# Routing attention and a SoLU feed-forward on one core: the first pair of heads prepared by thirds of its tokens, in a new written order

## The chip, the cores and the metric

The kernel runs on one core of one Trainium2 chip. The metric is the device time of one execution in microseconds (us); less is better. A core has TensorE (PE in the profile, its weight loads PEld), VectorE (DVE), ScalarE (ACT), GpSimd (POOL) and SyncE (SP), which here only issues DMAs. Each engine works through its own instructions in the order in which they were written and waits for the others by semaphores.

## The reference

q, k and v have 4 batches, 8 heads, 768 tokens and 64 numbers a head. Each query and each key is given the nearest of 16 centroids of its head; a query attends only to keys with its own centroid. The result, 3072 rows of 512, goes through a feed-forward block.

```python
q_assign = argmax(einsum('bhsd,hcd->bhsc', q_n, c_n)); k_assign = ...   # normalised rows
mask = q_assign[..., :, None] == k_assign[..., None, :]
attn = softmax(where(mask, q @ k.T / 8, -1e9));  x = attn @ v           # per batch and head
h = x @ w_in;  solu = h * softmax(h)
out = (solu - mean) / sqrt(var + 1e-6) * g_ln @ w_out
```

## The kernel before

**Layout.** Heads go in pairs: 4 batches x 4 pairs. For a pair, `qk` holds for queries and for keys 64 rows of numbers and, beneath them, rows with the one-hot of the token's centroid, so that one product gives the score and, where the centroids agree, a large constant, which the exponential's bias takes off again. `scores` (L595, the matmul is L602) fills a PSUM bank `sps` of up to 512 columns, `expo` (L608) takes its exponential on ACT into `e`, `values` (L625) multiplies 128-column blocks of `e` by v with a column of ones, and `normalise` (L637, L650) divides on DVE into `x`. Rings of three score banks and nine `e` tiles tie the three engines together.

**A pair's preparation.** In batches 1 to 3 a pair is loaded in 128-byte runs and turned by DVE (L408). In batch 0 it is loaded with tokens on partitions, turned on PE (`turn_tokens`, L387) and copied out of PSUM (`keep_tokens`, L394; steps `tp` and `xa`). Then `cast` (L432 to L436, `ca`) writes bf16 rows into `qk`; `clusters` (L446, L451, `cl`) multiplies by the centroids; DVE turns the products (`turn_back`, L460, `tb`), takes the maximum (L473, `mx`), compares (L479, L485, `oh`), turns back (L492, L495, `ot`), and `place` (L507 to L515, `pl`) copies the one-hot rows into `qk`.

Pairs 1 to 3 of batch 0 ("apart") are loaded whole in 1536-byte runs, two neighbouring tokens lying side by side, so that after the turn one half of the partitions holds even tokens and the other odd tokens; their centroids `c_by_two` stand accordingly, and each head's one-hot takes 16 rows.

Pair 0 of batch 0 is the first work of all. It is taken by halves of its tokens (`halves_of`), each half of each head by a DMA of 96 KB in 256-byte runs, eight in all on the ACT and SP queues (L370). It uses the centroids `c_bd`, 32 one-hot rows copied twice, `blank` (L524) to clear one head's rows, and its scores are units of kind "C": 384 queries by 128 keys, 24 banks of 384 columns. All other units of batch 0 are of kind "A": 256 queries, banks of 512 columns.

The centroids are scaled on DVE (L843 to L856) after one `pow` on POOL, and turned on PE twice: step `cp` for `c_bd` (L876), and later `cq` for `c_by_two` (L869).

**Feed-forward.** For each of 24 tiles of 128 tokens: x is turned by DMA (`tx`, L680), four `h` steps (L711) multiply by w_in (loaded by `li`, cast by `wi`, L553), `hm` (L717, DVE maximum), `ex` (L723, ACT exponential), `u` (L730, DVE product), `tu` (L735, turned by DMA), `bn` and `ag` (L741, L745, DVE), `at` and `al` (L751 to L760, POOL), four `y` steps (L775) and `sc` (L790, L792). `ce` (L588) centres w_out once.

**What sets the order.** Every step is added to a list by `add` with an engine, a cost, a due time, and what it needs. The order of each engine is not found by those: the strings `ORDER` name, engine by engine, the kinds of steps in sequence (S scores, E exponentials, V values, N normalise, ld, lv, lo and li loads of q/k, v, w_out and w_in, fl a filler matmul with no use for its result, and so on), and `AWAY` says which steps run on another engine than their first. `run` issues the steps in that order. PE begins with `wm`, six fillers of 512 columns (L820).

Of the kernel before, what the change touches and what calls it, by code (L numbers as in the profile page):

```python
# [22 lines left out]
class Weave:  # L23
# [6 lines left out]
        ld4 lv si ld4 lv lg ld4 lv2 ld4 lo2 ld4 lo ld3 lo ld3 li4 tx ld3 lv3 tx ld4 tu ld9 lv ld tu  # L30
        tx ld3 tu ld3 ou ld2 ou ld tu ld12 tu ld4 lv ld2 ou tx ld3 tu ou ld2 tx lv ld tu ld4 tx ld
        tu ou2 ld lv ld4 tu ld4 tu ld ou ld7 pl ou ld lv2 ld3 tu lv tx ou tu lv pl ld4 ou2 tx lv tu
        tx ou tu pl2 tu2 tx tu tx ou2 tx ou tu tx2 ou tu2 ou2 tu2 ou6
    """
    ORDER["POOL"] = """
        po z ca2 pl2 cv z bl pl2 ca z ca pl2 ca z2 ca3 cv ca cv ca pl3 sg ca cv2 pl3 ca2 gs pl ca cv
        ca wi ca pl2 wi3 bl ca pl2 cv at cv pl ca pl al bl at cv ca pl ca pl cv ca3 al at ca al ca
        at ca pl2 bl cv pl2 ca4 at ca2 al ca pl2 bl pl2 cv2 ca3 al at pl2 bl pl2 ca pl al ca3 at cv
        at pl ca pl2 ca2 pl al cv2 bl cv2 pl2 ca pl al pl at al at pl2 ca3 at al bl cv pl2 bl cv2
        ca3 pl5 al cv3 at al ca2 cv ca cv ca2 at ca2 pl ca al pl2 at2 pl3 at ca cv al at2 al2 at2 al  # L40
        at al3 at al2 at2 al2
    """
    ORDER["PE"] = """
        wm tp2 cp tp cl tp fl5 cl fl4 S3 tp2 S2 tp S cq S tp S2 tp2 S2 V3 S cl S tp2 V3 S gt S tp S
        tp S2 cl S2 V2 S V S2 tp S2 tp S2 V2 S V S2 cl S2 V2 S V2 S3 V S2 V2 S2 V S cl S3 su S2 V3 S
        V S3 V3 S2 V S su S2 V S V3 S3 me S3 V4 S3 cl S3 V4 S2 h S h S2 h S h S2 V3 S2 V h S h V S V
        S h S V S V S h S2 V3 S2 V h S2 h V2 S y3 S2 h3 S3 y V3 h V S2 V2 S cl S3 h2 S2 V3 S y2 S V
        h2 S V y2 S h S V h S2 h S y3 S2 y V3 h S3 cl V2 S V S y S2 y2 S3 V3 S y S2 V3 S2 cl S V S2
        V2 S h S2 V2 S V S h S2 V2 cl V2 S3 y2 S V S2 V y S2 y V2 S3 h2 S V h S h S2 V h S V S V y2
        S h V y2 S2 V S h3 S cl V S2 V2 S h V cl S3 h2 V y V S3 y2 V S h V3 S y S h S2 h2 S3 V2 y h  # L50
        S V S2 y V3 y S3 h3 y S3 V3 S h S V S V cl S V S h S cl V2 S3 y V2 S y S2 y V2 S3 h y V S3 V
        h V2 S3 cl S2 V2 S y3 S2 y S V3 S V S y S2 V S V3 S2 y2 S3 y V2 S2 h V2 S3 h3 S V S2 V y S V
        h2 V2 S y S2 y V y S h2 S3 cl h V S2 V3 S h V2 S3 h2 S y S2 V h S2 V y2 V4 S3 y h S2 h V h V
        S V S y2 S3 V3 h2 S2 h2 S2 y2 S V S h2 S V3 S2 h S h S2 V S y V2 S V y2 S2 h2 S2 h2 V2 S2 V2
        y S2 h V2 h V S2 h S V h S3 V2 h y S V y3 V h3 S2 y3 S2 y h2 V2 h y h y3 h V h V y4 h ptx h
        y4 h2 y3 h2 y ptu2 y6 ptu y ptu y5
    """
    ORDER["DVE"] = """
        cn cb xa ca tb mx oh ot pl2 tb mx oh ot xa3 bl cf cv xa zo xa2 tb ca mx oh gk N ot tb pl mx
        xa2 oh xa cv N ot tb pl N xt mx xt N oh ot tb pl2 ca N pl xt mx N sk oh N ot xt ce3 N tb ce5  # L60
        N hm mx N u oh ot bn N bn ag hm xt2 u N bn2 hm ag sc xt u N bn tb hm mx bn oh ag u xt bn ot
        xt N cv hm bn ag sc xt tb mx N u xt oh ot sc N bn2 xt ag xt tb N hm mx tb N oh ot u xt mx N
        bn oh bn xt hm ot ag N cv u bn2 xt hm tb mx u N tb oh mx hm ot bn2 oh ag u N sc ag hm bn ot
        u bn N xt2 ag xt2 hm tb N bl mx tb bn2 oh u N xt ag xt sc hm ot tb mx oh N bn sc N u bn N ag
        xt ot bn ca N mx sc oh hm u bn ag N xt hm bn2 bl tb u ot ag N hm mx bn2 u bn N oh ot hm bl2
        u ag N cv hm sc bn u N hm ag bn N bn u bn2 hm ag2 N bn u bn2 N ag hm bn u N ag hm bn2 u bn2
        hm sc u N ag2 bn tx hm bn sc u bn ag hm bn tu ag u2 bn2 ag sc
    """
    ORDER["ACT"] = """
        wa xa2 ca2 xa ca2 E12 xa2 E6 xa E58 ex E12 ex E8 ex E8 ex E3 sc E5 ca E2 ex E25 ex E9 sc E6  # L70
        ex E5 sc E2 ex E9 ex E8 ex E9 sc E6 ex E18 ex E21 ex E5 sc E3 ex E9 ex E7 sc E2 ex E7 ex E8
        ex E7 ex E6 sc E ex E2 sc E3 ex E2 sc ex sc ex sc ex tu sc tu2 sc2 oz
# [3 lines left out]
        ca0.0.0.0.0 ca0.0.0.1.1 ca1.3.1.1 sc23.0 tu22.1 tu23.1 xa0.0.1.0 xa0.2.1.0 xa0.2.1.1  # L76
        xa0.3.0.0
    """.split(), "ACT"))
    AWAY.update(dict.fromkeys("""
        bl0.0.1 bl2.2 bl3.1 bl3.2 bl3.3 ca0.0.1.0.0 ca0.1.1.0 ca1.0.0.1 ca3.1.1.0 cv0.0.0 cv0.2.0  # L80
        cv1.2.0 cv2.0.0 cv3.3.0 pl0.0.0.1.1 pl0.1.0.0 pl0.2.1.1 pl0.3.0.0 pl0.3.0.1 pl0.3.1.0 sc0
        sc10 sc13 sc17 sc19 sc2 sc23.1 sc3 sc6 sc8 sc9 tu22.0 zo
    """.split(), "DVE"))
    AWAY.update(dict.fromkeys("""
        ca0.0.1.1.1 pl0.0.0.1.0 pl0.0.1.0.0 pl0.0.1.1.0 pl1.0.0.0 pl1.0.0.1 pl1.0.1.0 pl1.0.1.1
        pl1.1.0.0 pl1.1.0.1 pl1.1.1.0 pl1.1.1.1 pl1.2.0.0 pl1.2.0.1 pl1.2.1.0 pl1.2.1.1 pl1.3.0.0
        pl1.3.0.1 pl1.3.1.0 pl1.3.1.1 pl2.0.0.0 pl2.0.0.1 pl2.0.1.0 pl2.0.1.1 pl2.1.0.0 pl2.1.0.1
        pl2.1.1.0 pl2.1.1.1 pl2.2.0.0 pl2.2.0.1 pl2.2.1.0 pl2.2.1.1 pl2.3.0.0 pl2.3.1.0 pl2.3.1.1
        pl3.0.0.0 pl3.0.0.1 pl3.0.1.0 pl3.0.1.1 pl3.1.0.1 pl3.1.1.0 pl3.1.1.1 pl3.2.0.0 pl3.2.0.1
        pl3.2.1.0 pl3.3.0.1 pl3.3.1.0 pl3.3.1.1  # L90
# [79 lines left out]
def kernel(  # L170
# [15 lines left out]
    P = 128  # L186
# [5 lines left out]
    QTR = S // 4  # L192
# [89 lines left out]
    for b in range(B):  # L282
        for p in range(n_pair):
            a, c = 2 * p, 2 * p + 1
            if (b, p) == (0, 0):
                for s in range(2):
                    GROUPS.append([unit(b, "C", h, s) for h in (a, c)])
                BANKS.extend((n, kt) for half in range(2) for n in GROUPS[0]
                             for kt in range(3 * half, 3 * half + 3))
                for n in GROUPS[1]:  # L290
                    in_order(n)
# [64 lines left out]
    def apart(b, p):  # L356


        return by_token(b) and not halves_of(b, p)

    def halves_of(b, p):
        return (b, p) == (0, 0)

# [19 lines left out]
    def turn_tokens(b, p, i, hf):  # L383

        j = tps[b, p, i, hf]
        for t in range(n_t // 2):
            uses(nc.tensor.transpose(hreg[:, j, t * P:(t + 1) * P],  # L387
                                     tokens(b, p, i)[:, hf * (n_t // 2) + t, :], ident_f[:]), j)
# [20 lines left out]

    def side(b, p, i, hh, cols):  # L410

        both = qk[slot(b, p)][:, i * 2 * S:(i + 1) * 2 * S]
        if not halves_of(b, p):
            return both.rearrange("p (h n) -> p h n", h=2)[:, hh, cols]
        f = cols.start // HALF
# [845 lines left out]
```

## Time and profile before

| what | value |
|---|---|
| time, median of 3 runs | 224.27 us (223.94 to 225.0) |
| the profiled execution | 223.91 us |
| its span, first to last instruction | 221.9 us |
| granted PE clock | 1.00 |
| HBM read, written | 23.11 MB, 6.29 MB |
| steps on PE | 294 score banks, 192 value groups, 96 h, 96 y |

The span is what the profile covers; the 2.0 us around it are not in it. In the profile a line such as L602 is a line of the kernel printed above; `out<-in` are tiles by name; x3 counts instructions. PE's busy time is modelled from its starts, so short waits can hide in it. An engine's idle time is put down to whatever released it last.

### The profile page before, as it was taken

What the parts mean: (1) busy time and instruction counts of PE and PEld (TensorE: products, weight loads), DVE (VectorE), ACT (ScalarE), POOL (GpSimd) and SP (SyncE); (2) the same over time, 40 slices, a digit from 0 to 9 for tenths busy, and PEclk for the clock granted to TensorE, in tenths of its full rate; (3) what the DMA queues carried; (4) which work ended last, traced back from release to release, by engine and by line L of the source; (5) the groups of instructions that cost most, each with busy time, mean ns of one, the idle gap of its engine ahead of it and who ended that gap; (6) DMA issues with size and microseconds to landing.
All of it is one profiled execution on the core that took longest, in us unless ns stands there. A gap on an engine that the chain in (4) does not pass through costs nothing.

```text
span 221.9 us, 6576 instructions
## 1 busy us (share of the span) xinstructions
PE 213.1 (96%) x2388; PEld 146.3 (66%) x2420; DVE 197.2 (89%) x359; ACT 191.7 (86%) x372; POOL 127.1 (57%) x247
## 2 busy tenths in 40 slices
PE   7899999999999999999999999999999999999994
PEld 2575656677667678776577666777677777755452
DVE  3899898899999999999998999887999889888982
ACT  3689999999899999998889899999899998983363
POOL 3499842954794999547668534953895403022331
PEclk9999999999999999999999999999999999999999
DMA  6997999999897989899999898499930524396723
GB/s 150 337 324 157 244 226 296 277 237 161 141 214 134 218 140 168 193 193 173 187 240 150 153 184 207 90 171 240 227 74 11 97 57 135 85 136 166 177 80 142
DMA packets 125679, 38.80 MB, mean 175 GB/s; under 512 B 115016, under 2 KB 121168, under 8 KB 125648
## 3 DMA queue, kind: packets, MB, share of 16 engines
q1 hardware_dynamic: 123904, 37.87, 80.4%
q10 hardware_dynamic: 1744, 0.52, 1.0%
q8 instruction: 19, 0.31, 0.6%
q14 instruction: 12, 0.10, 0.1%
HBM read 23.11 MB, written 6.29 MB: 132 GB/s over the span
## 4 chain that ended last, share of the span: by engine, by line
PE 83%; ACT 6%; issue 3%; DVE 2%; DMA 2%; POOL 1%; SPq 1%; ACTq 0%; DVEq 0%; POOLq 0%
PE sps L602 27%; PE hreg L711 17%; PE yps L775 17%; PE ops L625 13%; ACT e L608 5%; PE csc L451 4%; DMA raw<-in_q_dram 2%; PE hreg L387 1%; PE hreg L575 1%; PE hreg L775 1%; PE csc L446 1%; DVE u L730 1%; SPq L370 0%; PE utp L699 0%; ACT xt L394 0%
## 5 line engine op out<-in xcount | busy, mean ns | idle before, releaser
L608 ACT ACTIVATE e<-sps 128x512 bf16<-128x512 f32 (+1 forms) x294 | 150.7, 601 | 11.6 <-PE sps L602 9.6
L602 PE MATMUL sps<-qk 80*128 80x256 bf16 (+5 forms) x636 | 94.2, 264 | 2.0 <-POOL qk L515 0.7
L602 PEld LDWEIGHTS <-qk 80*128 80x128 bf16 (+1 forms) x636 | 60.3, 121 | 28.3 <-issue 9.2
L625 PEld LDWEIGHTS <-e 128*128 128x128 bf16 x1152 | 49.2, 97 | 12.3 <-issue 1.9
L625 PE MATMUL ops<-v,e 128*128 128x65 bf16 x1152 | 53.5, 193 | 0.1
L711 PE MATMUL hreg<-w_in_sb,xT 128*128 128x512 bf16 x173 | 49.1, 379 | 1.1
L775 PE MATMUL yps<-w_out_c,uT 128*128 128x512 bf16 x171 | 46.6, 379 | 0.6
L730 DVE TENSOR_TENSOR u<-e_sb,hreg 128x1024 bf16<-128x1024 bf16 (+1 forms) x25 | 29.1, 1168 | 4.8 <-ACT e_sb L723 4.5
L515 POOL COPY qk<-oht 32x384 f32<-32x384 f32 (+1 forms) x50 | 24.4, 488 | 15.6 <-DVE oht L495 13.4
L741 DVE BATCH_NORM_STATS2 bs<-u 128x6 f32<-128x512 bf16 x48 | 31.5, 677 | 0.1
L717 DVE TENSOR_REDUCE nmax<-hreg 128x1 f32<-128x1024 f32 x24 | 29.0, 1208 | 2.5 <-PE hreg L711 2.2
L723 ACT ACTIVATE e_sb<-hreg,nmax 128x1024 bf16<-128x1024 f32 x24 | 26.9, 1123 | 4.5 <-DVE nmax L717 4.4
L434 POOL CAST qk<-xt 64x768 bf16<-64x768 f32 (+1 forms) x31 | 25.9, 837 | 4.8 <-DVE xt L394 3.3
L775 PEld LDWEIGHTS <-uT 128*128 128x128 bf16 x200 | 18.2, 97 | 11.7 <-issue 0.3
L757 POOL TENSOR_SCALAR esq<-es,mv 128x1 f32<-128x1 f32 x24 | 8.5, 355 | 28.9 <-DVE mv L745 20.7
L436 POOL TENSOR_SCALAR qk<-xt 64x768 bf16<-64x768 f32 (+1 forms) x28 | 22.8, 815 | 1.7
L711 PEld LDWEIGHTS <-xT 128*128 128x128 bf16 x192 | 16.7, 97 | 9.5 <-DVE u L730 0.6
L408 DVE STREAM_TRANSPOSE xt<-raw 128x768 f32<-128x768 f32 x24 | 22.7, 953 | 0.2 <-DMA w_g<-in_moe_w_out_dram 0.2
L751 POOL TENSOR_SCALAR es<-esum 128x1 f32<-128x1 f32 x24 | 5.3, 222 | 27.5 <-ACT e_sb L723 27.0
L650 DVE TENSOR_TENSOR x<-ops,den 128x256 bf16<-128x256 f32 (+1 forms) x39 | 19.0, 486 | 1.3
L760 POOL TENSOR_TENSOR alpha<-esq,halves 128x1 f32<-128x1 f32 x24 | 13.5, 561 | 2.0
L533 POOL CAST v<-vf 128x384 bf16<-128x384 f32 x27 | 13.5, 516 | 0.9 <-DMA vf<-in_v_dram 0.2
(80 smaller groups left out, 165.6 us busy)
## 6 DMA issues: line engine op xcount, KB each, us to landing
vf<-in_v_dram SPq DMA_DIRECT2D x16, 384.0 KB, 4.7
out_dram<-y SPq DMA_DIRECT2D x23, 256.0 KB, 2.6
raw<-in_q_dram SPq DMA_DIRECT2D x50, 96.0 KB, 3.3
raw<-in_k_dram SPq DMA_DIRECT2D x50, 96.0 KB, 2.9
w_g<-in_moe_w_out_dram SPq DMA_DIRECT2D x4, 512.0 KB, 4.6
w_st<-in_moe_w_in_dram SPq DMA_DIRECT2D x4, 512.0 KB, 5.9
raw<-in_q_dram SPq DMA_DIRECT2D x3, 384.0 KB, 6.2
raw<-in_k_dram SPq DMA_DIRECT2D x3, 384.0 KB, 6.7
```

The costliest lines, as they stand in the source:

```text
L434: VEC[e].tensor_copy(dst, src)
L436: VEC[e].tensor_scalar(dst, src, scalar1=inv_C, scalar2=1.0, op0=Alu.mult, op1=Alu.mult)
L515: ins = VEC[e].tensor_copy(dst.bitcast(F32), src.bitcast(F32).unsqueeze(1) .to_broadcast([NB, 2, n // 2]))
L602: nc.tensor.matmul(sps_[n, k][:, c0:c0 + w], side(b, h // 2, 1, h % 2, keys)[r], side(b, h // 2, 0, h % 2, slice(s0 * P, s0 * P + w))[r])
L608: nc.scalar.activation(es[n, k][:, :w], sps_[n, k][:, :w], Act.Exp, scale=exp_scale, bias=-exp_scale)
L625: nc.tensor.matmul(opss[g][:, s, :VW], es[n, k][:, c0:c0 + P], v1[slot(b, h // 2)][:, h % 2, kt, :VW], start=(kt == 0), stop=(kt == n_t - 1))
L711: uses(nc.tensor.matmul(hreg[:, at(f, f2)[1], :], xTs[f][:, dc, :], w_in_sb[:, dc, f2 * FF2:(f2 + 1) * FF2], start=(dc == 0), stop=(dc == ...
L717: uses(nc.vector.tensor_reduce(ff[f, "nmax"][:], pair_of(f), axis=AXY, op=Alu.max, negate=True), *both(f))
L723: uses(nc.scalar.activation(ff[f, "e"][:], pair_of(f), Act.Exp, bias=ff[f, "nmax"][:], accum_out=ff[f, "esum"][:]), *both(f))
L730: uses(nc.vector.tensor_tensor(ff[f, "u"][:, at_], ff[f, "e"][:, at_], pair_of(f)[:, at_], op=Alu.mult), *banks)
L741: nc.vector.bn_stats(ff[f, "bs"][:, f2, :], ff[f, "u"][:, f2, :])
L775: ins = nc.tensor.matmul(dst, ff[f, "uT"][:, at(f, f2)[0] * (n_fc // 2) + c, :], w_out_c[:, fc, cols], start=(fc == chunks[0]), stop=(fc = ...
```

## The change

- Pair 0 of batch 0 takes the layout of pairs 1 to 3 ("apart" is now all of batch 0), by thirds of its tokens (256 tokens of each head): six loads of 128 KB in 512-byte runs, queries on the ACT queue and keys on SP's. Each third is turned by two transposes for queries and two for keys, copied, cast, multiplied by the centroids (128 columns) and given its one-hot separately. Its rows are placed for each head once (16 rows); nothing is blanked.
- Its scores become units of kind "A": 18 banks of 512 columns, in an order that uses the first third first.
- The centroids are turned once, into PSUM's `ops` bank; `c_by_two` is written for the first two heads (`cf0`) and then the others (`cf1`), then `c_bd` (`cb`). The root's correction is arranged in other steps. The first values wait for these three.
- `wm` is 20 fillers of 128 columns, and all fillers are of 128; there are 24 `fl` in place of 9, eight of them after the first scores.
- ORDER and AWAY are new for every engine, over the whole kernel. On DVE: 12 casts `ca` (before 4), 12 v casts `cv` (5), 7 scalings `sc` (11), no `bl` (5), one `wi` (0). On ACT: 9 copies `xa` (6), 18 `sc` (14). On SP: no `pl` (4), and `li` after 15 issued `ld` (before 22).

The core of the diff:

```diff
     def apart(b, p):
-        return by_token(b) and not halves_of(b, p)
-    def halves_of(b, p):
+        return by_token(b)
+    def by_thirds(b, p):
         return (b, p) == (0, 0)
...
-    def load_tokens(b, p, i, hh, t0, t1, eng):
+    def load_third(b, p, i, c, eng):
...
-        eng.dma_start(out=tokens(b, p, i)[:, t0:t1, hh * D:(hh + 1) * D],
-                      in_=SRC[i][b, 2 * p + hh].rearrange("(p t) d -> p t d", p=P)[:, t0:t1, :])
+        eng.dma_start(out=raws[b, p, i][:].rearrange("p j c -> p (j c)")
+                      .rearrange("p (h t e) -> p h t e", h=2, t=n_t // 2)[:, :, c, :],
+                      in_=SRC[i][b, 2 * p:2 * p + 2].rearrange(
+                          "h (p t u) d -> p h t (u d)", p=P, u=2)[:, :, c, :])
...
-                for s in range(2):
-                    GROUPS.append([unit(b, "C", h, s) for h in (a, c)])
+                for s in range(n_t // 2):
+                    GROUPS.append([unit(b, "A", h, s) for h in (a, c)])
+                (a0, c0), (a1, c1), last_two = GROUPS
+                BANKS.extend([(a0, 0), (c0, 0), (a0, 1), (c0, 1), (a1, 0), (a1, 1),
+                              (a0, 2), (c0, 2), (a1, 2), (c1, 0), (c1, 1), (c1, 2)])
...
-    add("wm", "PE", 3.55, -1000, lambda e: [idle(FF2) for _ in range(6)])
+    add("wm", "PE", 3.55, -1000, lambda e: [idle(P) for _ in range(20)])
...
-    add("cp", "PE", 0.42, 0, lambda e: turn_centroids(), ["cn"], take="m")
-    add("cb", "DVE", 0.27, -500, lambda e: keep_centroids(), ["cp"], give="m")
-    add("cq", "PE", 0.28, 0, lambda e: turn_centroids(), ["cn"], ["cp"], take="m")
-    add("cf", "DVE", 0.4, -490, lambda e: keep_by_two(), ["cq"], give="m")
+    add("cp", "PE", 0.22, 0, lambda e: turn_centroids(), ["cn"])
+    add("cf0", "DVE", 0.2, -500, lambda e: keep_by_two(0, 2), ["cp"])
+    add("cf1", "DVE", 0.35, -490, lambda e: keep_by_two(2, H), ["cp"])
+    add("cb", "DVE", 0.27, -480, lambda e: keep_centroids(), ["cp"])
```

The new orders begin (the first stretch of each):

```python
PE:  wm fl4 tp2 fl2 tp cp fl3 tp cl tp cl tp fl5 cl fl2 S fl S tp fl2 tp S2 tp S fl tp S tp2 S cl S tp ...
DVE: cn xa cf ca2 tb mx oh tb ot mx pl oh pl ot tb ca pl xa mx pl oh ot cf xa2 ca cb tb xa mx oh N ...
ACT: wa xa4 ca xa ca3 E2 xa E xa E xa E5 xa E61 ex ...
POOL: ca zo ca3 pl2 cv pl2 ca pl sg pl2 z ca cv ca pl ca pl ca pl2 ca cv ...
```

More of the change, by code (lines that the diff above doesn't have):

```diff
@@ L46 @@
[L46 to L50, printed above, removed]
@@ L913 @@
                 last_tp.append(f"tp{t}.{hf}")
-                e = "ACT" if (b, p) == (0, 0) and i == hf else "DVE"
-                costs = {"ACT": 0.4, "DVE": 0.475}
-                add(f"xa{t}.{hf}", e, costs[e], first - 14 + i + hf,
+                costs = {"ACT": 0.28, "DVE": 0.33} if third else {"ACT": 0.4, "DVE": 0.475}
+                add(f"xa{t}.{hf}", "DVE", costs["DVE"], first - 14 + i + hf,
                     (lambda e, b=b, p=p, i=i, hf=hf: keep_tokens(b, p, i, hf, e)),
@@ L1002 @@
             for j, (i, part) in enumerate(hots):
-                e = ("DVE", "POOL")[j % 2] if half else "POOL" if apart(b, p) else "SP"
-                costs = ({"DVE": 0.3, "POOL": 0.41} if half else
+                e = ("DVE", "POOL")[j % 2] if third else "POOL" if apart(b, p) else "SP"
+                costs = ({"DVE": 0.2, "POOL": 0.3} if third else
                          {"POOL": 0.76, "DVE": 0.46} if apart(b, p) else
```

313 lines of the change are left out of this document (168 added, 145 removed).

## The prediction

> **What bounds the kernel now.** The first views are the page's busy line and busy time by stage. In the stage rows each engine has its busy us and, in brackets, its instructions.
>
> ```profile
> PE 213.1 (96%) x2388; PEld 146.3 (66%) x2420; DVE 197.2 (89%) x359; ACT 191.7 (86%) x372; POOL 127.1 (57%) x247
> ```
>
> ```profile
> 20.00:40.00 20.00, 19.26 (x260) 12.52 (x257) 18.13 (x38) 18.98 (x40) 12.15 (x21) 1.00 0.93 242
> 40.00:60.00 20.00, 19.35 (x236) 14.15 (x238) 18.82 (x34) 19.53 (x39) 13.09 (x23) 1.00 1.03 195
> 60.00:100.00 40.00, 39.62 (x465) 28.65 (x471) 38.66 (x66) 38.02 (x74) 29.11 (x51) 1.00 0.95 180
> 100.00:140.00 40.00, 39.56 (x448) 27.23 (x453) 38.01 (x66) 36.21 (x70) 24.93 (x48) 1.00 1.00 183
> 140.00:180.00 40.00, 39.41 (x470) 29.18 (x477) 34.56 (x60) 38.03 (x74) 24.55 (x45) 1.00 0.60 122
> ```
>
> Once the flow stands PE is the bound: 39.62, 39.56 and 39.41 us busy of 40 in three stages. So a gain can only come from three places: the stretch before real scores run, waits that PE's busy time hides in the first 40 us (where ACT is at 18.98 of 20 and DVE at 18.13), or the tail. The view that carries the first is the chain of waits up to the first score (start, duration, engine, tile, line):
>
> ```profile
> 5.81 0.53 PE hreg L387 x3
> 6.37 0.56 DVE xt L394
> 6.93 0.26 DVE qk L436
> 7.19 0.30 DVE cst L460
> 7.51 0.36 DVE mx L473
> 7.90 0.43 DVE oh L485
> 8.36 0.39 DVE oht L495
> 8.88 0.36 POOL qk L515
> 9.29 0.35 POOL qk L515
> 9.68 0.65 PE sps L602 x3
> ```
>
> The reader is to see that the first score waits for DVE, not for PE or the loads: DVE copies a turned half, casts it, takes the one-hot of the other half (transpose, maximum, compare, transpose), and POOL places two rows one after the other. The new code changes just this stretch.
>
> **The change part by part.** *The first score.* DVE starts on it when the centroids' rows are scaled, the last row here. The other rows price the new, smaller steps (mean ns of one):
>
> ```profile
> 4.48 0.29 DVE L856 TENSOR_SCALAR w_in_sb<-c_all,c_inv 128x128 f32<-128x128 f32 x1
> ```
>
> ```profile
> L460 DVE STREAM_TRANSPOSE cst<-csc 128x384 f32<-128x384 f32 x15 | 8.6, 572 | 1.4 <-PE csc L451 1.1
> L460 DVE STREAM_TRANSPOSE cst<-csc 128x192 f32<-128x192 f32 x2 | 0.8, 376 | 0.0
> L473 DVE TENSOR_REDUCE mx<-cst 128x12 f32<-128x192 f32 x2 | 0.7, 353 | 0.1
> L485 DVE TENSOR_TENSOR oh<-cst,mx 128x192 bf16<-128x192 f32 x2 | 0.8, 390 | 0.1
> L495 DVE STREAM_TRANSPOSE oht<-oh 128x192 bf16<-128x192 bf16 x2 | 0.8, 380 | 0.1
> L394 DVE COPY xt<-hreg 128x384 f32<-128x384 f32 x10 | 5.1, 538 | 0.4 <-PE hreg L387 0.4
> L436 DVE TENSOR_SCALAR qk<-xt 64x384 bf16<-64x384 f32 x1 | 0.3, 344 | 0.0
> L515 DVE COPY qk<-oht 32x192 f32<-32x192 f32 x2 | 0.5, 272 | 0.1
> ```
>
> The transposes give about 1.02 ns an element over a fixed 0.18 us (192 to 384 elements: 376 to 572 ns). With that slope a third costs, as estimates: transpose (128 wide) 0.31, maximum 0.29, compare 0.33, transpose back (now 256 wide, with gaps) 0.44, copy of a turned third 0.41, cast 0.27, one placed row 0.20; the centroids' first two heads (64 wide) 0.22. DVE's new order from the scaled centroids at 4.77 us to the first score's last row is: copy, centroids, two casts, transpose, maximum, compare, transpose of the second third, transpose back, maximum of the second third, one placed row: 0.41+0.22+0.54+0.31+0.29+0.33+0.31+0.44+0.29+0.20 = 3.34 us, with 0.02 us between steps 3.55, so 8.35; the score then begins at about 8.45 instead of 9.68: **1.2 us earlier**. POOL's row of the keys runs beside DVE's maximum and row. Bounds: if the first third is turned 0.4 us later than the centroids are ready, 0.8; at best 1.4.
>
> [...] If steps shrank in proportion to width, the four of a third would come to about 1.1 us and not the 1.37 taken here.
>
> *Loads.* Eight loads of 96 KB become six of 128 KB in 512-byte runs. The chain leaves the loads at 5.81, and the new first score needs the first two loads only, so their price is hidden behind the centroid chain to 4.77. Cover gone, it costs the lateness of the first keys' third. SP issues one load fewer, so all later loads are issued sooner.
>
> *ACT.* Before, ACT's first exponential starts at 10.04:
>
> ```profile
> 10.04 3.56 ACT L608 ACTIVATE e<-sps 128x384 bf16<-128x384 f32 x9 [1.11 <-PE sps L602]
> 19.14 0.49 ACT L394 COPY xt<-hreg 128x384 f32<-128x384 f32 x1
> 19.60 5.62 ACT L608 ACTIVATE e<-sps 128x384 bf16<-128x384 f32 x12
> 25.38 5.50 ACT L608 ACTIVATE e<-sps 128x512 bf16<-128x512 f32 x11 [0.16 <-PE sps L602]
> ```
>
> Now ACT has five thirds to copy and four to cast first (about 0.37 and 0.40 each, 3.5 us from 4.8, and a wait for the last third), so it is free near 9.0, 1.0 us earlier. Pair 0's scores become 18 banks of 512 in place of 24 of 384: 18 x 0.50 = 9.0 us against 24 x 0.395 = 9.5. With four copies of 0.46 between (before three, and some waits) pair 0 ends at about 9.0+9.0+1.8 = 19.8, against 19.60+6x0.395 = 22.0 before. That is 2 us ahead, if nothing else holds.
>
> *But DVE holds it.* Pair 3 of the batch can't be scored before its one-hot, and DVE leads there by nothing. Rows of before:
>
> ```profile
> 30.73 0.98 DVE L492 STREAM_TRANSPOSE w_out_c<-w_out_c 128x768 bf16<-128x768 bf16 x1
> 32.20 1.26 DVE L507 COPY qk<-w_out_c 16x384 f32<-16x384 f32 x2
> 33.71 1.10 PE L602 MATMUL sps<-qk 80*128 80x256 bf16 x6
> ```
>
> Adding the mean durations of DVE's instructions from the scaled centroids through this transpose gives 25.9 us before and 27.5 after (three short chains for two, more casts). Before, they took 26.9 us (4.77 to 31.71), so at least 1.0 us of that was waiting; more, since neighbours overlap (the cast of 344 ns fills 0.26 us of the chain). If no wait is left and nothing overlaps, the new order ends at 32.3; at the pace of 0.96 that such overlaps give, at 31.2. I take 31.6, against 31.7: two POOL rows of about 0.55 follow, and pair 3's scores begin at about 32.7 against 33.7. That is **1.0 us ahead** at this point (0.3 to 2.0).
>
> *Centroids turned once, fillers, bank counts.* One transposition of 0.11 us leaves PE. 24 fillers of 128 columns replace 9 of 256. Before:
>
> ```profile
> 7.11 0.71 PE L820 MATMUL idle_p<-w_out_c 128*128 128x256 bf16 x5
> ```
>
> That is 0.11 each past the first's latency, so about 0.055 for 128 columns; eight now stand among the first scores: 0.45 us if PE were the path, 0 while it waits for ACT. I take 0.1 after the saved transposition. Score columns are the same (24 x 384 = 18 x 512).
>
> *Written order, loads.* The four loads of w_in now stand seven 96 KB loads further forward in SP's queue. Before, POOL waits for them:
>
> ```profile
> 38.87 1.04 POOL L553 CAST w_in_sb<-w_st 128x1024 bf16<-128x1024 f32 x1 [3.95 <-DMA w_st<-in_moe_w_in_dram]
> ```
>
> At the 242 GB/s of that stage 0.67 MB is 2.8 us. PE had scores to do meanwhile and idled only 0.65 us between 40 and 60 us, so the gain lies between 0 and 0.65; I take 0.3. The chunk loads that fall behind belong to batch 1's second pair, whose scores come after those of a whole other pair.
>
> *Written order, DVE.* DVE takes six more full casts, seven more v casts and one w_in cast, and gives up four scalings and five blankings:
>
> ```profile
> L533 DVE CAST v<-vf 128x384 bf16<-128x384 f32 x5 | 2.2, 441 | 0.0
> L434 DVE CAST qk<-xt 64x768 bf16<-64x768 f32 x1 | 0.7, 742 | 0.0
> L436 DVE TENSOR_SCALAR qk<-xt 64x768 bf16<-64x768 f32 x2 | 1.1, 570 | 0.0
> L792 DVE TENSOR_SCALAR y<-yps,alpha 128x512 f32<-128x512 f32 x10 | 7.3, 735 | 0.9 <-issue 0.5 <-POOL alpha L760 0.2 <-PE yps L775 0.2
> L524 DVE MEMSET qk<- 16x384 f32 x4 | 1.5, 378 | 0.4
> ```
>
> 6x0.65 + 7x0.44 + 0.95 - 4x0.735 - 5x0.35 = +3.2, and with the third chain and smaller items about +4.2 us of DVE work. Where it lies matters. Counting along both orders, up to the maximum of token tile 12 (batch 2's first) the new order has only about 0.9 us more DVE work (though PE has five output quarters less to do before that tile). The rest falls behind 150 us, where DVE idles 5.4 of 40 us. It can cost 0 (hidden) to 3.5 (all of it on the path, since 60 to 140 has only 3.3 us idle); I take 0.1.
>
> *Tail.* 20 output quarters remain after the last value group against 24, and seven quarters of the first product against six; PE is filled there. Both halves of the last scaling now run on ACT: about +0.1.
>
> **Sum** against the profiled execution (span 221.9 us and 2.0 around it, 223.91 in all, 0.36 under the median 224.27): -1.2 for the first score, of which 0.2 is lost at pair 3; -0.3 for w_in; -0.1 for the longer ACT lead; +0.1 fillers; +0.1 DVE; +0.1 tail: -1.1. That is 222.8; I state **222.7**, inside the rounding of these terms. The order is new everywhere, so its own range is 221.3 to 223.8.
>
> **The rivals.**
> 1. *The head start is eaten.* DVE is the path from 10 to 33 us and ends pair 3's one-hot when it did before, or a little later. For it: 27.5 against 25.9 us of work. Against it: the waits that vanish. Time: 223.91 + 0.1 + 0.1 + 0.1 with no gain, 224.2.
> 2. *Slower: DVE becomes the bound of the middle.* Between 60 and 140 us DVE has 3.3 us idle in 80, and the first product of a tile waits for the product u two tiles earlier on DVE. Once moved casts run ahead of a maximum or a u by more than that idle, PE stands still. It decides from about 3 us of extra DVE work before tile 12, where I count 0.9 by itself, but nearer 3 measured against PE's own progress. Price 2.5 to 3.5 less the 1.1 gained: 225.3 to 226.3; I say 225.8.
> 3. *The new order removes more.* ACT's 2 us lead holds because pair 3's rows come earlier (32.5), and w_in gives its full 0.65: 221.9 - 2.6 + 2.0 = 221.3, down to 220.5.
> 4. *The clock.* PE starts slow:
>
> ```profile
> 1.17 2.74 PE L820 MATMUL idle_p<-w_out_c 128*128 128x512 bf16 x6 [1.17 <-DVE halves L824]
> ```
>
> That is 0.43 us for 512 columns, half the later pace (0.11 for 256). If PE fell back to it for one stretch as long (2.7 us) after the scores begin, that costs up to 1.4, which eats the gain: 224.2. Against it: ACT, not PE, paces that stage.
>
> [...]
>
> **How the numbers follow.** Forecast 0.45 (221.3 to 223.8), rival 3 0.14, rival 1 0.20, rival 2 0.18, rival 4 0.03. The range leaves out the far end of rival 3 and the upper half of rival 2: 220.9 to 225.6. About 0.5% (1.1 us) is what a measurement of this kernel can tell from no change. Faster than 223.15: rival 3 and four fifths of the forecast, 0.50; slower than 225.4: 0.18; within: 0.32.
>
> **What would show it.** The first score at 8.3 to 8.9 and the first exponential near 9.0; pair 0's exponentials done at 20; the transpose of pair 3's one-hot at 31 to 32 and its scores half a microsecond to one earlier than 33.7; POOL's w_in casts 2 us or more sooner; DVE busy up by 4 us in all and PE's idle time in 60 to 140 not over 1.5 us. The prediction is wrong if the first score starts after 9.2, if pair 3 starts after 33.7, or if PE's idle time in the middle grows by over 1 us.

## The result, and the profile after

The changed kernel takes **239.31 us** (median of 4 runs, 238.73 to 239.93), the kernel before beside it 224.46 (223.94 to 225.0): a ratio of 1.0662, 95% interval 1.0623 to 1.0701. It is 15 us slower, far outside the range. The profiled execution took 239.93, with a span of 238.0. Times in this document are medians of all executions; ratios and their intervals leave out the few executions (at most one in four of a changed kernel) that fell into a slower state of the chip, so that a time and its ratio need not match to the last digit.

The busy time by stage, in the columns of the prediction's stage rows (PE, PEld, DVE, ACT, POOL, the granted clock, the DMA engines' busy share, GB/s):

```profile
20.00:40.00 20.00, 19.01 (x255) 12.22 (x252) 18.02 (x36) 17.60 (x33) 15.56 (x27) 1.00 0.86 249
40.00:60.00 20.00, 18.27 (x236) 13.28 (x236) 18.28 (x32) 18.80 (x38) 10.51 (x16) 1.00 0.75 124
60.00:100.00 40.00, 35.66 (x406) 24.61 (x408) 34.77 (x59) 35.00 (x68) 24.97 (x45) 1.00 1.12 179
100.00:140.00 40.00, 35.75 (x414) 26.14 (x421) 35.09 (x62) 33.45 (x65) 23.23 (x43) 0.99 1.08 178
140.00:180.00 40.00, 39.57 (x422) 27.20 (x426) 36.85 (x62) 35.84 (x69) 22.76 (x43) 0.97 0.67 135
```

The reader is to see that no engine became the bound of the middle. From 60 to 140 us PE, DVE, ACT and POOL are all less busy than before: PE stands still for 8.59 of 80 us (before 0.82), DVE works 69.86 us (before 76.67). These 80 us hold less of the work than before. Over the same work, from batch 1's first exponential to batch 3's, DVE is busy 92.6 of 104.8 us (before 90.6 of 95.0): it has 2.0 us more to do, but 9.8 us more pass. The engines wait for one another. PE's waits from 40 to 140 us (what waits, for what: total, times, longest), first of before and then of after:

```profile
PE sps L602 <- ACT e L608: 0.3, 1, 0.3
```

```profile
PE hreg L729 <- DVE u L748: 2.2, 1, 2.2
PE yps L793 <- DMA uT<-u: 2.2, 2, 1.6
PE ops L643 <- DVE x L668: 1.6, 2, 1.3
PE hreg L729 <- DMA xT<-x: 1.4, 1, 1.4
PE csc L464 <- ACT y L808: 1.1, 1, 1.1
```

And behind them the waits of DVE, SP (its queue of DMA issues) and ACT in the same stretch:

```profile
DVE den L655 <- PE ops L643: 4.1, 3, 1.7
DVE xt L430 <- DMA raw<-in_q_dram: 3.1, 2, 2.9
```

```profile
SPq L698 <- DVE x L668: 13.6, 1, 13.6
```

```profile
ACT y L808 <- DMA out_dram<-y: 1.0, 1, 1.0
```

There is no common releaser: a product u, a turned u, a turned x, a division and a store, each late once or twice, by up to 2.2 us. SP's long wait is the eye-catcher: it stands at the first turn of x from 29.7 to 43.3 us with loads queued behind.

Where the time is lost is seen best by the same work's start in both traces. This table (us, worked out from the starts of ACT's exponentials in the traces, in the columns also those of five experiments below) follows single scores:

| first exponential of | before | after | thirds, then before's order | before, then after's order | after, long runs | before's first, after's order, long runs |
|---|---|---|---|---|---|---|
| all | 10.0 | 9.7 | 9.6 | 10.1 | 9.3 | 10.9 |
| pair 1 | 22.1 | 23.8 | 22.8 | 22.2 | 23.4 | 23.0 |
| pair 3 | 34.8 | 38.2 | 36.6 | 35.2 | 37.8 | 36.0 |
| batch 1 | 51.8 | 56.1 | 53.6 | 52.7 | 55.7 | 53.4 |
| batch 2 | 98.1 | 108.8 | 99.8 | 103.9 | 104.1 | 101.6 |
| batch 3 | 146.8 | 160.9 | 148.6 | 154.4 | 152.8 | 149.9 |
| end of span | 221.9 | 238.0 | 223.8 | 231.3 | 230.4 | 226.5 |

After starts 0.3 us early, is 1.7 late at pair 1, 4.3 at batch 1, 10.7 at batch 2 and 14.1 at batch 3. So there are two losses: one of some 4 us up to batch 1's first scores, and a larger one through batches 1 and 2. Another 2.0 us come between batch 3's first exponential and the end (77.1 us against 75.1); PE is busy there for 72.2 us against 70.9, so about 1.4 of them are work that the new order leaves for later. The columns with after's order take 76.6 to 77.6 us for this stretch, run 3's 75.2. Since the new order puts the h and y steps elsewhere between the scores, one such lag by itself can be off by a few us: that of the last column falls from 3.5 us at batch 2 to -0.7 45 exponentials later, and is 3.1 again at batch 3.

In the first one, ACT's timeline (start, duration, instruction; in brackets its idle time and what ended it) shows the form of the loss:

```profile
9.74 1.09 ACT L626 ACTIVATE e<-sps 128x512 bf16<-128x512 f32 x2
10.93 0.48 ACT L416 COPY xt<-hreg 128x384 f32<-128x384 f32 x1
11.31 0.60 ACT L626 ACTIVATE e<-sps 128x512 bf16<-128x512 f32 x1
11.80 0.48 ACT L416 COPY xt<-hreg 128x384 f32<-128x384 f32 x1
12.15 0.63 ACT L626 ACTIVATE e<-sps 128x512 bf16<-128x512 f32 x1
13.58 0.48 ACT L416 COPY xt<-hreg 128x384 f32<-128x384 f32 x1 [0.80 <-PE hreg L405]
```

Copies of turned queries stand singly between exponentials, and on PE the turns stand singly between scores. With three score banks, score, turn, copy, exponential and next score form one chain, and each link waits for the other engine.

### The profile page after: what moved, and what is told of

It is laid out like the page before. It is cut to its first block, busy times and chain, and to the rows that moved or that the text cites. A ratio compares the mean times of both kernels' runs of the same rounds, so it can differ in the third digit from the quotient of the medians.

```text
span 238.0 us, 6680 instructions
## 1 busy us (share of the span) xinstructions
PE 218.8 (92%) x2437; PEld 150.8 (63%) x2468; DVE 203.8 (86%) x372; ACT 196.4 (83%) x374; POOL 124.7 (52%) x246
## 3 DMA queue, kind: packets, MB, share of 16 engines
q1 hardware_dynamic: 122800, 37.67, 79.9%
## 4 chain that ended last, share of the span: by engine, by line
PE 45%; DVE 18%; DMA 14%; ACT 7%; POOL 5%; issue 5%; SPq 4%; POOLq 0%; DVEq 0%; ACTq 0%
PE sps L620 13%; PE hreg L729 10%; PE yps L793 10%; PE ops L643 6%; ACT e L626 6%; DMA raw<-in_k_dram 5%; DMA raw<-in_q_dram 4%; DMA xT<-x 4%; DVE xt L430 4%; PE csc L464 3%; SPq L422 2%; DVE u L748 2%; DVE x L668 2%; DMA out_dram<-y 2%; PE hreg L405 2%
## 5 line engine op out<-in xcount | busy, mean ns | idle before, releaser
L626 ACT ACTIVATE e<-sps 128x512 bf16<-128x512 f32 x288 | 152.9, 605 | 21.3 <-PE sps L620 19.8
L620 PE MATMUL sps<-qk 80*128 80x256 bf16 (+3 forms) x648 | 99.8, 264 | 3.2 <-ACT e L626 1.7
L620 PEld LDWEIGHTS <-qk 80*128 80x128 bf16 (+1 forms) x648 | 61.8, 121 | 34.5 <-issue 12.5
L643 PEld LDWEIGHTS <-e 128*128 128x128 bf16 x1152 | 52.0, 98 | 14.4 <-DVE x L668 2.1
L643 PE MATMUL ops<-v,e 128*128 128x65 bf16 x1152 | 56.7, 194 | 1.8 <-DVE x L668 1.6
L793 PE MATMUL yps<-w_out_c,uT 128*128 128x512 bf16 x173 | 49.0, 379 | 2.8 <-DMA uT<-u 2.2
L759 DVE BATCH_NORM_STATS2 bs<-u 128x6 f32<-128x512 bf16 x48 | 31.6, 673 | 0.1
L534 POOL COPY qk<-oht 32x384 f32<-32x384 f32 x48 | 25.4, 530 | 12.0 <-DVE oht L510 5.8
L453 POOL CAST qk<-xt 64x768 bf16<-64x768 f32 (+1 forms) x26 | 20.7, 798 | 16.8 <-DVE den L655 6.5
L793 PEld LDWEIGHTS <-uT 128*128 128x128 bf16 x200 | 17.5, 98 | 10.9 <-DMA uT<-u 2.5
L455 POOL TENSOR_SCALAR qk<-xt 64x768 bf16<-64x768 f32 (+1 forms) x28 | 22.5, 803 | 2.1 <-DVE den L655 0.4
L808 ACT ACTIVATE y<-yps,alpha 128x512 f32<-128x512 f32 x16 | 11.2, 697 | 6.5 <-POOL esq L775 3.2
L551 POOL CAST v<-vf 128x384 bf16<-128x384 f32 x20 | 10.7, 536 | 4.1 <-DMA vf<-in_v_dram 3.5
```

Of the source, the lines that this page charges most:

```text
L534: ins = VEC[e].tensor_copy(dst.bitcast(F32), src[:, :n].bitcast(F32).unsqueeze(1) .to_broadcast([NB, 2, n // 2]))
L620: nc.tensor.matmul(sps_[n, k][:, c0:c0 + w], side(b, h // 2, 1, h % 2, keys)[r], side(b, h // 2, 0, h % 2, slice(s0 * P, s0 * P + w))[r])
L626: nc.scalar.activation(es[n, k][:, :w], sps_[n, k][:, :w], Act.Exp, scale=exp_scale, bias=-exp_scale)
L643: nc.tensor.matmul(opss[g][:, s, :VW], es[n, k][:, c0:c0 + P], v1[slot(b, h // 2)][:, h % 2, kt, :VW], start=(kt == 0), stop=(kt == n_t - 1))
L759: nc.vector.bn_stats(ff[f, "bs"][:, f2, :], ff[f, "u"][:, f2, :])
L793: ins = nc.tensor.matmul(dst, ff[f, "uT"][:, at(f, f2)[0] * (n_fc // 2) + c, :], w_out_c[:, fc, cols], start=(fc == chunks[0]), stop=(fc = ...
```

## The experiments

Every experiment changes the written order, or the runs of the loads; the arithmetic of the kernel is the same unless it says otherwise. Ratios are to the kernel before, measured beside it on the same chip; intervals are 95%.

**1. Loads ahead of the first turns of x.** The first theory was that the loss begins with SP's 13.6 us.

```diff
-SP: ... ld li4 tx ld6 lv ld2 tx ld4 tu ...
+SP: ... ld li4 ld6 lv ld2 tx2 ld4 tu ...
```

> The changed kernel, whole, but on SP the first two x transposes (tx0, tx2) stand behind the eight loads that follow them in the changed kernel's order, so that the 13.6 us in which SP waits for x at 29 to 43 us has loads issued ahead of it. Theory A (the loss begins with SP standing at tx0 in front of loads): the loads come some 13 us earlier, the wait of 2.19 us for raw at 45 us and part of the later ones go; 230 to 236 us. Theory B (the loss is spread over the whole written order, of which tx0 is one place): 236 to 239. Theory C (DVE's extra work bounds the middle, the recorded second rival): no change, 238 to 240.

239.53 us, 1.0646 (1.0568 to 1.0724). Nothing is regained, though the eight loads now go out from 27 to 41 us. The hole only moves: the DMA engines' share is 1.01 at 35 to 40 us, where it was 0.28, and 0.50 at 50 to 55, where it was 1.13. Theory A falls in this form. The time is also what theory C (DVE's extra work) had forecast; against that theory stand DVE's busy times above, and run 7 below.

**2. All loads as early as before.** Every load of q, k and v stands behind no more transposes and stores than in the kernel before.

```diff
-SP: ... li4 tx ld6 lv ld2 tx ld4 tu ld4 lv ld4 lv tu tx ld7 tu ...
+SP: ... li4 ld7 tx lv ld3 lv2 tx ld4 tu ld10 lv tu tx ld3 tu ...
```

> The changed kernel, whole, but on SP every load of q, k and v stands behind no more transposes and stores than it does in the kernel before; the order of transposes and stores, and of all other engines, is the changed kernel's. Theory A (late loads are the cause): 226 to 233 us. Theory B (the written order of the other engines is matched to its own SP order, and is itself what costs): 236 to 241, since a load pulled ahead waits for its buffer and holds up the transposes behind it. Theory C (DVE's extra work): 238 to 240.

241.42 us, 1.0748 (1.067 to 1.0827): a little slower. With the loads early (share 1.11 at 35 to 40 us) DVE waits 11.3 us for PE's values from 40 to 140 us (4.1 in after). Where SP puts the loads isn't the cause by itself.

**3 and 4. Layout and order apart.** Two kernels are put together at the end of the first pair's scores: the layout by thirds with its first stage, and then the order of before on all engines; and the mirror of it.

```diff
 # 3, all engines
+up to the first pair's scores: loads, layout and order of after
+from there: ORDER and AWAY of before
 # 4, all engines
+up to the first pair's scores: loads, layout and order of before
+from there: ORDER and AWAY of after
```

> The layout by thirds, its loads, its centroids and the changed kernel's order of all engines up to the end of the first pair's scores; from there the order and the placement of work on engines of the kernel before, on all five engines (SP's whole order but the first loads is that of before); three idle matmuls fewer. It tells the layout with its first stage from the rest of the written order. If the rest of the order costs most of the 15 us: 225 to 228 us (the first stage's lateness of 1.7 us at the 18th exponential kept, no more added). If the layout itself costs it (DVE's extra work, or the first stage's delay growing through the middle): 233 to 240.

> The mirror of the run before: the kernel before with its own first pair, loads and centroids and its own order up to the end of the first pair's scores; from there the order and placement of the changed kernel on all engines (SP's from the last value load of batch 0 on). If the rest of the written order is the cost: 233 to 240 us. If the layout is: 222 to 227.

Run 3: **226.10 us**, 1.0073 (1.0035 to 1.0111). Run 4: **233.49 us**, 1.0367 (1.0281 to 1.0452). The rest of the order is most of the loss, and it costs on the old layout too. In run 3 the middle is whole again; PE's waits of run 3 and then of run 4, 40 to 140 us, with the stage row of 60 to 140 of each:

```profile
PE sps L571 <- ACT e L577: 0.2, 1, 0.2
...
60.00:140.00 80.00, 79.23 (x897) 55.69 (x910) 76.44 (x129) 74.09 (x143) 54.46 (x98) 1.00 1.18 182
```

```profile
PE hreg L673 <- DVE u L692: 2.9, 2, 1.6
PE yps L737 <- DMA uT<-u: 1.6, 1, 1.6
PE ops L587 <- DVE x L612: 1.2, 3, 0.6
PE hreg L673 <- DMA xT<-x: 0.5, 1, 0.5
...
60.00:140.00 80.00, 72.76 (x846) 51.28 (x856) 72.97 (x125) 70.30 (x135) 51.59 (x91) 1.00 0.96 184
```

PE stands 0.77 us in run 3 and 7.24 in run 4, with the waits of the changed kernel. And in run 3 DVE has the whole new preparation of the first pair before it, yet the 1.8 us by which it is behind at pair 3 are the 1.8 at batch 3: once the order has slack, an early delay neither grows nor shrinks.

**5. Switching in the middle.** The order of after until about 64 us, then that of before.

```diff
+up to about the 80th exponential: ORDER and AWAY of after
+from there: ORDER and AWAY of before
```

> The changed kernel in its own order on all engines up to about the 80th exponential (near 64 us), from there the order and placement of the kernel before. At that place the changed kernel is 4.3 us behind. If the loss of each stretch is made by the order of that stretch: 228 to 230 us, the 4.3 us kept and no more added. If the early order leaves a backlog (loads and transposes late) that goes on costing: 232 to 236.

234.78 us, 1.0403 (1.0303 to 1.0503). By the ratios, the 4.3 us are kept and some 5 more are lost in the good order. In the profile the lag is 5.7 us at the 81st exponential (PE's granted clock had fallen once, at 48.4 us; 0.91 from 40 to 60 us), 10.4 at batch 2's first, and from the 153rd on it stays at 10.9 to the end. So the early order goes on costing for a while after it has ended, as a backlog would; behind the switch PE's longest waits are for turned x and u (1.8 and 0.8 us).

**6. One knot undone.** The longest wait of PE, 2.21 us for u at 135.6 us, came from a transposition on DVE that waited for its load and stood ahead of that u. It is the twentieth of 24 in DVE's order, so the keys of batch 3's second pair, not of the first as the expectation has it.

```diff
-DVE: ... xt(batch 3, pair 1, keys) ag u(tile 8) ca ...
+DVE: ... ag u(tile 8) xt(batch 3, pair 1, keys) ca ...
```

> The changed kernel with one move: on DVE the product u of tile 8 stands ahead of the transposition xt (keys of batch 3's first pair) that waited for its load at 131 to 135 us, instead of behind it. In the changed kernel PE then waited 2.21 us for u, and 3.4 us of half clock followed at 139 us. If the waits are single knots of the order: the wait and the half clock go, 234.5 to 236.5 us. If the next wait takes the place (uT, xT or the keys late instead): 238 to 239.5.

239.65 us, 1.0624 (1.0545 to 1.0702): nothing. That wait for u is gone, but others take its place (2.0 us for a turned x, 1.1 before a y step), and PE's clock falls at 47.8 and 109.3 us (0.51 and 0.50 in the next 3.4 us) instead of at 139.2. The knots are not independent.

**7 and 8. Shorter transfers, and the control.** The loads of batches 1 to 3 bring the same bytes in 3 KB runs instead of 128-byte runs; tokens then lie elsewhere in the tile, so the output isn't the reference's, but each instruction, tile size and wait remains.

```diff
-            in_=SRC[i][b, 2 * p + c // 2, :, (c % 2) * NB:(c % 2 + 1) * NB]
-            .rearrange("(j i) c -> i j c", i=NB))
+            in_=SRC[i][b, 2 * p + c // 2].rearrange(
+                "(i t) d -> i (t d)", i=2 * NB)[(c % 2) * NB:(c % 2 + 1) * NB]
+            .rearrange("i (j c) -> i j c", c=NB))
```

> The changed kernel, its order untouched, but the 96 loads of q and k for batches 1 to 3 bring the same bytes in contiguous runs of 3 KB instead of 128 bytes, so that the tokens lie in the tile in another order and the output isn't the reference's; every instruction and wait stays. Theory D (the order costs because loads and transposes come later from the DMA engines than the order allows for; raw, uT, xT late): 226 to 233 us. Theory E (the order of PE and DVE itself makes them wait for each other, whatever the DMA does): 236 to 240.

> The control of the run with long runs: the kernel before with the same edit (the 96 loads of q and k of batches 1 to 3 in runs of 3 KB, so that the output isn't the reference's). Its PE waits for no transfer between 40 and 140 us. If the long runs helped the changed kernel only because its order leaves no slack for late transfers: 223 to 225 us, no gain. If they lighten any kernel (ports, queues): 216 to 220, the same 6 us.

The changed kernel: **233.15 us**, 1.0343 (1.0265 to 1.042). The kernel before: 224.13 us, 0.9957 (0.9919 to 0.9995). The same relief gives the changed kernel 6 us and the old one next to nothing. Here is the main DMA queue's row of after, and then of after with long runs (packets, MB, share of 16 engines' span), with PE's waits of the latter from 40 to 140 us:

```profile
q1 hardware_dynamic: 122800, 37.67, 79.9%
```

```profile
q1 hardware_dynamic: 52144, 37.67, 67.4%
...
PE ops L644 <- DVE x L669: 1.6, 2, 1.3
PE yps L794 <- DMA uT<-u: 0.8, 1, 0.8
PE hreg L730 <- DMA xT<-x: 0.2, 1, 0.2
```

The waits for u, for the store and most of those for turned x and u are gone, without one instruction moved: PE stands still for 1.8 us from 60 to 140 us, where it stood for 8.6. From batch 1's first exponential to batch 3's it now takes 97.0 us, with the same DVE work (92.4 us busy). So DVE's work is not what costs there, and a large part of the loss is transfers that come later than the order allows for. Two things stay unseparated. The edit also shortens SP's issue of such a load, from 0.52 to 0.42 us, while the median time from issue to landing goes only from 4.0 and 3.5 us (q and k) to 3.6 and 3.5; so whether the late ones were issued late or carried slowly isn't shown. And in this profile PE's clock doesn't fall in the middle (1.00 from 60 to 140 us), which alone can be up to 1.7 us. For the same 37.67 MB the queue's share of the engines' span is 79.9% with the short runs and 67.4% with the long ones.

**9. Batch 1's second pair back in its place.** Its loads ahead of w_in's, its two turns on DVE near 36 and 39 us.

```diff
-SP:  ... lv ld li4 tx ld6 lv ld2 tx ...
+SP:  ... lv ld8 li4 ld tx lv tx ...
-DVE: ... tb ot mx oh pl ot N sk ca cv N2 wi ca ce2 N ce5 xt N ce hm xt N u ...
+DVE: ... tb ot xt mx oh pl ot xt N sk ca cv N2 wi ca ce2 N ce5 N ce hm N u ...
```

> The changed kernel with the place of batch 1's second pair put back to about where the kernel before has it: its seven loads stand ahead of the four loads of w_in on SP (not behind them and tx0), the first load of the third pair ahead of tx0, and its two transpositions xt on DVE behind the one-hot turns of pair 3 and of batch 1's first pair (near 36 and 39 us instead of 50.7 and 53.9). If the late start of this pair is what leaves the DMA engines idle at 40 to 50 us and late afterwards: 230 to 235 us, and PE's losses from the 36th to the 180th exponential shrink. If the lack of slack is all along the order: 237 to 241.

242.63 us, 1.0803 (1.0702 to 1.0904): 3.3 us more. The two turns delay a division x at once (PE waits 2.2 us for it at 38.9 us, and its clock falls at 42.0; 0.70 from 40 to 45 us). In the profile it is 3.4 us behind the changed kernel at batch 2 and 1.3 at batch 3: part comes back, but not more than was lost. This too is no single cause.

**10 and 11. The rest of the two-by-two with long runs.** The same loads in the kernels of runs 4 and 3.

> The kernel before up to the end of its first pair, the changed kernel's order from there, and the 96 loads of q and k of batches 1 to 3 in runs of 3 KB (output not the reference's). With short runs this order cost 9.2 us. If late transfers are most of what the order costs by itself: 225 to 228 us. If they cost only together with the late first stage: 230 to 233.

> The layout by thirds with the changed kernel's first stage, the kernel before's order from there, and the long runs (output not the reference's). With short runs it was 226.1, 1.8 us over before. If that is the work of the first 24 us (DVE, POOL, copies on ACT): 225.5 to 226.5 us, no gain. If it is late loads: 224 to 224.8.

Run 10: **228.47 us**, 1.0148 (1.0082 to 1.0214). Run 11: **226.52 us**, 1.0074 (1.0045 to 1.0102). Half of what the order costs by itself is late transfers; nothing of what stays with the layout is. All eight together, as ratios to the kernel before:

| first pair | rest of the order | 128-byte runs | 3 KB runs |
|---|---|---|---|
| halves | before | 1 | 0.9957 |
| thirds | before | 1.0073 | 1.0074 |
| halves | after | 1.0367 | 1.0148 |
| thirds | after | 1.0662 | 1.0343 |

With 224.3 us to the unit: the first stage by thirds costs 1.6 us, the rest of the order 8.2, both together 14.8, so 5.0 arise only together. With long runs the order costs 4.3 (1.0148 over 0.9957) and both 8.7 (1.0343 over 0.9957). So about 6 of the 15 us go with the shorter transfers. Of the 8.7 that stay, 4.3 belong to the order alone, 2.6 to the layout with its first stage (1.0074 over 0.9957), and 1.8 arise only together. The intervals leave the single terms about 1 to 2 us of room, and those that arise only together more than 2.

**12 and 13. The first stage.** Can the 1.8 us of run 3 be ordered away? First one copy on ACT, the one with the 0.80 us wait; then the first 30 us of four engines.

```diff
 # 12, on run 3
-ACT: ... E xa(pair 1) E xa(pair 1) E xa(pair 2) E2 ...
+ACT: ... E xa(pair 1) E xa(pair 1) E E2 xa(pair 2) ...
 # 13, on run 3: PE, beginning of the scores
-PE:  S fl S tp fl2 tp S2 tp S fl tp S tp2 S cl S tp S2 tp V4 ...
+PE:  tp2 S tp fl S tp fl2 S tp S2 tp fl S tp S2 cl S2 V tp V ...
```

> The run with the layout by thirds and the rest of the order of before, with one move on ACT: the copy of the first half of pair 2's turned queries stands two exponentials later, where ACT stood 0.8 us before it at 12.6 to 13.4 us with a score already waiting. If that stand is what the first stage loses: 225.0 to 225.5 us. If PE's own order holds the next score back: 226 us as without the move.

> The run with the layout by thirds and the rest of the order of before, with the first 30 us of PE, DVE, ACT and POOL reordered: turns ahead of scores, copies on ACT behind exponentials that are ready, four casts and copies on other engines. If the 1.8 us of the first stage are order too and not layout: the 36th exponential near 31.5 us as in the kernel before, 224 to 225 us. If the layout itself costs it (DVE and POOL have more to do): 226 to 228.

Run 12: 228.26 us, 1.0103 (0.9992 to 1.0214), inconclusive: in its profile pair 1 does come 0.9 us earlier (21.9), but at 97.7 us PE waits 2.2 us for a turned x, and then loses half its clock for 3.4 us (0.50 from 101.2 to 104.6). Run 13: 227.60 us, 1.0132 (1.0054 to 1.0209): pair 1's first exponential at 22.6, and the 0.9 us gained by pair 3's neighbourhood (32.4 against 33.3 at the 36th exponential) are lost again by batch 1 (54.3 against 53.6). The first stage's cost was not removed; whether it can be is open. No version with the reference's output beat the kernel before.

## Why the prediction was wrong, point by point

- **The first score, 1.2 us earlier.** It came 0.4 earlier: 9.31, not 8.45, past the bound of 9.2. DVE's steps were sized well (transpose, maximum, compare, transpose back: 0.32, 0.29, 0.29 and 0.40 us against 0.31, 0.29, 0.33 and 0.44; only the casts, 0.28 and 0.39 against 0.27 each, came out longer). What failed is that DVE alone was added up: it now needs PE twice in that chain, as the idle times in its timeline show (0.77 and 0.35 us).

```profile
4.67 0.42 DVE L416 COPY xt<-hreg 128x256 f32<-128x256 f32 x1
5.87 0.23 DVE L889 TENSOR_TENSOR w_out_c<-cps,own 128x64 f32<-128x64 f32 x1 [0.77 <-PE cps L885]
...
7.10 0.32 DVE L474 STREAM_TRANSPOSE cst<-csc 128x128 f32<-128x128 f32 x1 [0.35 <-PE csc L464]
```

POOL's row, which was to run beside DVE's, comes last: it stands behind a cast on POOL, and the score starts as its first copy ends.

```profile
8.49 0.40 POOL L455 TENSOR_SCALAR qk<-xt 64x256 bf16<-64x256 f32 x1
8.95 0.65 POOL L521 COPY qk<-oht 16x128 f32<-16x128 f32 x2
9.31 0.39 PE L620 MATMUL sps<-qk 80*128 80x256 bf16 x2
```

- **Loads hidden.** Not quite: the chain that ends in the first scores now begins with the keys' first third, landed at 4.24, and PE's turns of it, not with the centroids.
- **ACT free near 9.0, pair 0 done at 19.8.** 9.74, and pair 1 begins at 23.8. The 18 exponentials and four copies took 14.0 us where 10.8 was added up. The rates were right (0.50 us each); the waits between copy, turn and score were taken as none. Run 12 shows one such stand of 0.8 us, and that moving it moves pair 1 by 0.9 in the profile.
- **DVE holds pair 3: transpose at 31.6, scores at 32.7.** The transpose ended at 35.92 and pair 3's first exponential came at 38.2 (before 34.8). DVE was busy 27.14 us from the scaled centroids to there (before 23.90): 1.6 us more work was forecast, 3.2 came, since steps took longer than their rows of before (the three large compares alone by 1.1 us, see below), and idle 4.0 us (before 3.0).
- **w_in sooner by 2 us or more.** POOL's first cast of w_in began at 38.43 instead of 38.87: it now waits behind POOL's own rows for pair 3, which wait for DVE. The gain of 0.3 wasn't there: from 40 to 60 us PE stands for 1.73 us, before 0.65. That loads fell behind w_in and the first turn of x was passed over in a clause; runs 1, 2 and 9 show that giving them their place back brings nothing by itself.
- **Written order, DVE: 0.1, bounds 0 to 3.5. This is the step that failed most.** It priced a wholly new order by the DVE work that it adds, with DVE's idle time as the upper bound. The order costs 8 us where DVE has the old first pair (run 4), and 13 with the new one (239.31 against 226.10). DVE's work did grow by more than was counted, by 6.6 us over the kernel (203.8 against 197.2) instead of 4.2, but only 2.0 of it lies between batch 1's first exponential and batch 3's, where 9.8 us were lost, and with long runs (run 7) the same work takes 97.0 us there. So most of the order's price is not DVE's work but transfers and hand-overs that come later than the next step needs them: 6 us go when the loads' runs are lengthened; that the rest is hand-overs between PE and DVE is argued, not shown. The prediction counted along one engine; whether laying the landing times of the trace of before along the new order would have shown the loss was not tried.
- **Clock, tail, fillers.** The fillers are too small to be told apart here. The last exponential's start is followed by 17.7 us instead of 22.5, as the smaller rest of output quarters has it, but that is work moved ahead, not saved: from batch 3's first exponential to the end it is 2.0 us more than before, where the tail's term was 0.1.
- **The rivals.** The slower one (DVE becomes the bound of the middle) had the sign, about an eighth of the size and the wrong mechanism: DVE did not become the bound, it was busy for 88% of the stretch from batch 1's first exponential to batch 3's, before for 95%. The first rival's head start was eaten, and more. The clock did fall back for one stretch (below; 0.50 for 3.41 us), but after PE had waited, and in the middle; it adds at most 1.7 us to the profiled execution. The one execution of four whose clock stayed at 1.000 took 238.73 us, the others 239.13 to 239.93. The mark set in the prediction, PE's idle time from 60 to 140 growing by over 1 us, was the right one: it grew by 7.8.

What stays open: which pairs of neighbours in the order carry the 4 us that long runs don't remove. In run 10 PE's waits from 40 to 140 us come to 2.5 us in all. Its lag in the profile is 1.6 us at batch 1 (0.9 of it from the first exponential on), 3.1 at batch 3 and 4.6 at the end, so no single stretch carries it.

## What to carry to other kernels

A new written order is a change by itself, and often a larger one than what it is written for: look at the slack between each step, its transfer and its consumer on every engine, and don't price it by the work it adds to one of them. When many small waits appear with different releasers, don't repair them singly; swap the whole order for the old one with the new layout kept, and shorten all transfers at once: runs 3, 4 and 7 told here what the four single repairs of the changed kernel (runs 1, 2, 6 and 9) could not. And where two or three engines hand small pieces to each other through a short ring, add the hand-overs up, not the pieces.

## What the runs showed of the hardware that was not expected

**PE's clock can fall in the middle of a kernel, behind 3.4 us in which PE was idle for much of the time.** Stage rows of after, in steps of 3.4 us; the granted clock is the third number from the end:

```profile
132.40:135.80 3.40, 3.17 (x40) 2.19 (x36) 0.51 (x2) 3.40 (x8) 1.70 (x4) 1.00 0.83 132
135.80:139.20 3.40, 1.27 (x18) 1.12 (x20) 3.37 (x7) 1.46 (x4) 2.29 (x5) 1.00 0.13 26
139.20:142.60 3.40, 3.40 (x36) 2.54 (x33) 2.94 (x6) 1.56 (x3) 3.24 (x5) 0.51 0.77 130
```

PE was busy 1.27 of 3.4 us, and the next 3.4 us ran at half clock, though PE was fully busy again; the clock is back at 1.00 from 142.65 us on, after 3.41 us at 0.50 (139.24 to 142.65). The traces show the same behind stretches of 3.41 us in which PE was busy for 1.40 us (run 1), 1.06 and 1.12 (run 2), 2.03 (run 5), 2.03 and 1.45 (run 6), 1.19 (run 9) and 1.24 (run 12). In runs 2 (from 71.8 us), 6 (from 47.8 and 109.3) and 12 (from 101.2) the granted clock was then 0.50 or 0.51 for 3.4 us; the rows of the others, which are longer, show 0.97 (run 1, 120 to 140 us), 0.91 (run 5, 40 to 60) and 0.70 (run 9, 40 to 45). In these stretches PE was not idle but a third to three fifths busy. The kernel before shows 1.00 over its whole span, and runs 3, 4, 7, 8, 10, 11 and 13 show it up to about the last 2 us of theirs.

No threshold can be read from this. The clock fell in runs 5 and 6 behind a stretch with 2.03 us of work at 45 to 48 us; after has the same order there and as little work (2.03 us from 44.43 to 47.84 us), and its clock stayed. In run 4 it stayed at 1.00 behind 1.91 and 1.94 us of work in 3.4 (82.9 to 86.3 and 130.7 to 134.1 us). What decides isn't shown. By these rows one fall costs up to 1.7 us, half of 3.41, as an estimate.

**Some DVE steps take up to 2.6 times as long beside POOL's casts.** The same scaled cast on DVE stands three times in the trace of after, with POOL at work beside the first two:

```profile
42.78 2.48 POOL L571 CAST w_in_sb<-w_st 128x1024 bf16<-128x1024 f32 x2
44.29 1.38 DVE L455 TENSOR_SCALAR qk<-xt 64x768 bf16<-64x768 f32 x1
98.05 1.10 DVE L455 TENSOR_SCALAR qk<-xt 64x768 bf16<-64x768 f32 x1
156.68 0.53 DVE L455 TENSOR_SCALAR qk<-xt 64x768 bf16<-64x768 f32 x1
```

It takes 1.38 us beside POOL's cast of w_in, 1.10 beside POOL's own casts of 64x768, and 0.53 at 156.68, where POOL is idle. Over all fifteen traces it takes 0.53 to 0.54 us with POOL idle (10 times), and 0.61 (at 15.90 us of before) to 1.38 where a POOL step of 768 or 1024 numbers a row overlaps it for more than 0.3 us (19 times). The compare of 128x384 behaves alike: 0.53 to 0.56 us with POOL idle (90 times, 14 of them in before and after), up to 1.13 beside such steps (1.09 at 24.72 us of after). So do the three compares of batch 0's pairs 1 to 3, first of after, then of before:

```profile
L493 DVE TENSOR_TENSOR w_out_c<-cst,mx 128x384 bf16<-128x384 f32 x3 | 3.0, 1015 | 0.1
```

```profile
L479 DVE TENSOR_TENSOR w_out_c<-cst,mx 128x384 bf16<-128x384 f32 x3 | 1.9, 636 | 0.0
```

In after each of the three has a scaled cast of POOL beside it (0.88, 1.09 and 1.08 us). In before one of them has POOL idle beside it (0.55 us) and the others POOL's casts or copies (0.60 and 0.76), so not every POOL step slows it as much. A new order thus also changes which steps meet, and the row of a step in one order needn't hold in the next. The traces show the slowing, not its cause.
